# Attention with soft mixture of experts: a batch's turned logits and exponentials made around the first head's values

## The chip, the cores and the metric

One core of a Trainium2 chip runs the whole program. The metric is the device time of one launch in microseconds, the median of several runs; the profile is one execution of the same program, with the hardware profiler on. Five engines work side by side, each through its own queue in order: PE (matrix multiply), DVE (VectorE), ACT (ScalarE), POOL (GpSimd) and SP (which issues DMAs here). They wait for each other by semaphores.

## The reference, cut to what matters

Causal attention with a decay per position over 8 batches of 8 heads, 576 positions, 64 values a head; its output is the input of a soft mixture of 8 experts with 32 slots.

```python
# attention, for each batch and head
scores = q @ k.T / sqrt(D) + cum[:, None] - cum[None, :]      # cum = cumsum(log f)
attn = softmax(where(causal, -1e9, scores))
x = (attn @ v)            # -> (4608, 512): rows are tokens, columns head x value
# soft mixture of experts
logits = x @ phi                                              # 4608 x 32
d = exp(logits - logits.max(0)); d /= d.sum(0) + 1e-9          # over all tokens
slot_input = d.T @ x
slot_out = each expert's two layers on its 4 slots
c = exp(logits - logits.max(1)); c /= c.sum(1) + 1e-9          # over the slots
out = c @ slot_out
```

## The kernel before

The work is written out by hand: the order of the program's lines is the order of each engine's queue. The main loop runs over g, a pair of heads (32 pairs, 4 to a batch). I call one turn of it a slot. A slot holds, for pair g, the exact scores of both heads (`s2`, PE, into three PSUM banks `ring` in turn), their exponentials (`expo`, ACT, into `PTS`), the causal masks (`causal`, POOL), the values (`s3`, PE, 25 small matmuls a head, which the trace counts as 50, into the banks `pv`), and the normalization (`norm`, DVE). Between them stand a first pass of scores for heads further ahead (`s1`, PE, into PSUM tiles `s`) and their row maxima (`tops`, DVE), and the rounding of the keys and queries of pair g + 3 (`round_k`, `round_q`, ACT, from `RAW` into `WA` and `YA`). `load_qk(g + 3)` at the slot's start brings `RAW`; POOL makes the low parts (`low_k`, `low_q`).

The mixture's work for batch b is spread over the four slots after the batch's last pair; `b, w = divmod(g - 4, 4)`, so w counts them. In w = 0 `logits` makes the 32 logits of the batch's tokens, slots on partitions. In w = 1 `weigh` copies them to the tile `LG`, `mgroup` and `mtop` reduce them to a maximum per slot (`row`), `mcast` spreads it over the partitions (four small matmuls on PE into a bank of `ring`, then L405 and L407 on DVE), `weigh2` makes the exponentials `EX` (ACT), `total` adds up their sum, and `tokens` turns logits and exponentials so that tokens are on partitions: two transpositions of `LG` and two of `EX` on PE into the PSUM tile `tk`, and a copy of the turned exponentials to `LD` (ACT). L407 writes the negated maximum to column 192 of `LG`, which the second transposition of `LG` reads (columns 128 to 255). In w = 2 `combine(b, 0)` reduces and subtracts the row maximum of the turned logits (L475, L476, DVE, from `tk`), and `dispatch` multiplies the exponentials with x (PE). In w = 3 the other steps of `combine` follow.

`tk`, the tiles `s` and the logits take the three PSUM buffers of the pool `ps_s` in turn, in the order of the program. Three allocations after `tk` comes the tile of `s1(u0, 0)` of the next slot, so that matmul has to wait until everything that reads `tk` is done. All the dependencies are kept by the tile framework, for `tk` as one tile: a write to it waits for earlier reads of any part of it.

The end of a w = 1 slot, in order, before the change: the last `s1` and `s2`, `mcast`, `round_k`, `weigh2` and `total`, `round_q`, `s3` and `norm` of the first head, `s3` of the second head, `tokens`; the second head's `norm` comes in the next slot, and behind it `combine(b, 0)`.

Of the kernel before, what the change touches and what calls it, by code (L numbers as in the profile page):

```python
# [15 lines left out]
B, H, S, D = 8, 8, 576, 64  # L16
# [56 lines left out]
def attn_softmoe(ctx: ExitStack, tc: tile.TileContext, qk, v, f, phi, w1, w2, cst, out):  # L73
# [71 lines left out]
    st = {}  # L145
# [13 lines left out]
    def scratch(late, name):  # L159

        return turn() if late else ps_s.tile([P, 512], F32, name=name, tag="s")

    def turn():
        ring.append(ring.pop(0))
        return ring[-1]
# [10 lines left out]
    def round_k(g, *hs):  # L176
        if pair(g):
            for h in hs or range(2):
                nc.scalar.copy(WA[g % 3][0:64, S * h : S * h + S], RAW[g % 3][64:128, h])  # L179
# [35 lines left out]
    def s1(i, *which):  # L215

        if not head(i):
            return
        g, h = divmod(i, 2)
        ya, wa, m = YA[g % 3], WA[g % 3][:, S * h : S * h + S], TOP[g % 3]  # L220
        for n in which:
            bank, o, blk, j0, w = TOPS[n]
            if o == 0:
                st["top", i % 2, bank] = scratch(False, f"s{i}_{bank}")
            t = st["top", i % 2, bank]
            nc.tensor.matmul(  # L226
                t[:, o : o + w], ya[0:m, h, 128 * blk : 128 * blk + 128], wa[0:m, j0 : j0 + w], start=True, stop=True
            )
# [34 lines left out]
    def s2(i, *which):  # L263
        if not head(i):
            return
        g, h = divmod(i, 2)
        ya, wa, yb, wb, m = YA[g % 3], WA[g % 3], YB[g % 2], WB[g % 2], TOP[g % 3] + 1
        for n in which:
            bank, c, i0, w = SEGS[n]
            t, at = (turn(), 0) if n < 4 else st["bank"]  # L270

            n = 128 if c < 4 else 64
            o = t[0:n, at : at + w]
            at += w
            j0 = S * h + 128 * c
            nc.tensor.matmul(o, wa[0:m, j0 : j0 + n], ya[0:m, h, 64 + i0 : 64 + i0 + w], start=True, stop=False)  # L276
            nc.tensor.matmul(o, wb[:, j0 : j0 + n], yb[:, h, i0 : i0 + w], start=False, stop=True)  # L277
            st["bank"] = t, at
# [120 lines left out]
    def mcast(b):  # L399
        if not batch(b):  # L400
            return
        pm = turn()
        for j in range(4):
            nc.tensor.matmul(pm[32 * j : 32 * j + 32, 0:2], row, ones[0:1], start=True, stop=True)
        nc.vector.tensor_copy(st["mb", b][:, 1:2], pm[:, 0:1])  # L405
        if b < B - 1:
            nc.vector.tensor_scalar_mul(LG[:, 192:193], pm[:, 0:1], -1.0)  # L407
# [23 lines left out]
    def tokens(b, *ns):  # L431

        if not batch(b):
            return
        pm = turn() if b == B - 1 else scratch(False, f"tk{b}")
        for n in ns:
            src = (LG, EX)[n]
            nc.tensor.transpose(pm[:, 160 * n : 160 * n + 128], src[:, 0:128], ident)
            nc.tensor.transpose(pm[:, 160 * n + 128 : 160 * n + 256], src[:, 128:256], ident)
        if 0 in ns:  # L440
            st["tok", b] = pm
        if 1 in ns:
            copy = nc.scalar.copy if b < B - 1 else nc.vector.tensor_copy
            copy(LD, pm[:, 160:320].rearrange("p (t s) -> p t s", t=NBLK))
# [21 lines left out]
    def combine(b, step):  # L466

        if not batch(b):
            return
        ce = ctok[:, b]  # L470
        if step == 0:

            lt = st["tok", b][:, 0 : NBLK * NS].rearrange("p (t s) -> p t s", t=NBLK)
            sm = st["sm", b] = const.tile([P, 2, NBLK], F32, name=f"sm{b}", tag="sm", bufs=1)
            nc.vector.tensor_reduce(sm[:, 0], lt, axis=AX.X, op=ALU.max)  # L475
            nc.vector.tensor_tensor(ce, lt, wide(sm[:, 0]), op=ALU.subtract)  # L476
        elif step == 1:
            st["ce"] = turn()
            nc.scalar.activation(st["ce"][:, 0 : NBLK * NS].rearrange("p (t s) -> p t s", t=NBLK), ce, AF.Exp)
        else:  # L480
            sm, pm = st["sm", b], st["ce"]
            et, to = pm[:, 0 : NBLK * NS].rearrange("p (t s) -> p t s", t=NBLK), pm[:, NBLK * NS : NBLK * NS + NBLK]
            nc.vector.tensor_reduce(to, et, axis=AX.X, op=ALU.add)
            nc.vector.tensor_scalar_add(sm[:, 1], to, EPS)
            nc.vector.reciprocal(sm[:, 1], sm[:, 1])
            nc.vector.tensor_tensor(ce, et, wide(sm[:, 1]), op=ALU.mult)
# [208 lines left out]
    for g in range(1, NG):  # L695
        h0, h1 = 2 * g, 2 * g + 1
        u0, u1 = h0 + 3, h0 + 4
        b, w = divmod(g - 4, NPAIR)
        load_v(g + 1)
        if g > 0:  # L700
            load_qk(g + 3)
        if w == 1:
            weigh(b)
        low_q(h0 + 2)
        low_q(h1 + 2)
        s2(h0, 0)
        expo(h0, 0)
        norm(h0 - 1)
        if w == 1:
            mgroup(b)  # L710
        if w == 2:
            combine(b, 0)
        s1(u0, 2)
        tops(u0, 2)
        s2(h0, 1)
        expo(h0, 1)
        s1(u0, 3)
        tops(u0, 3)
        if g > 1:
            px(g - 1, 0)  # L720
        s2(h0, 2)
        expo(h0, 2)
        if g > 1:
            px(g - 1, 3)
        else:
            round_k(3, 0)
            round_q(3, 0)
        s1(u0, 0, 1)
        tops(u0, 0, 1)
        if g > 1:  # L730
            px(g - 1, 1)
        s2(h0, 3)
        if g > 1:
            xcopy(g - 1, (0,))
            xcopy(g - 1, (3,))
            px(g - 1, 2)
        s2(h0, 4)
        s1(u0, 4, 5)
        s2(h0, 5)
        expo(h0, 3)  # L740
        tops(u0, 4, 5)
        causal(h0)
        low_k(h0 + 2)
        if w == 1:
            mtop(b)
        s2(h1, 0)
        expo(h1, 0)
        if g == 1:
            for t in (0, 3, 1, 2):
                px(0, t)  # L750
            xcopy(0, (0,))
            xcopy(0, (3,))
        px(g - 1, 4)
        xcopy(g - 1, (1, 2))
        xcopy(g - 1, (4,))
        s1(u1, 2)
        tops(u1, 2)
        s2(h1, 1)
        expo(h1, 1)
        s1(u1, 3)  # L760
        tops(u1, 3)
        s2(h1, 2)
        expo(h1, 2)
        mturn(g + 1)
        mrows(g + 1)
        s1(u1, 0, 1)
        tops(u1, 0, 1)
        s2(h1, 3, 4)
        s1(u1, 4, 5)
        s2(h1, 5)  # L770
        expo(h1, 3)
        tops(u1, 4, 5)
        causal(h1)
        low_k(h1 + 2)
        if g == 1:
            round_k(3, 1)
            round_q(3, 1)
        load_cum(g + 3)
        dup_q(g + 2)
        dup_k(g + 2)  # L780
        if g == 29:
            sides[2].close()
            p2 = fresh(ctx, "p2", 2)
            wstream(RAW[30 % 3], *p2)
        if g == 30:
            sides[1].close()
            xp = ctx.enter_context(tc.tile_pool(name="xp", bufs=1))
            X.append(xp.tile([P, NBLK, 256], F32, name="X3"))
            p0 = fresh(ctx, "p0", 1)
            p1 = fresh(late, "p1", 3)  # L790
            wstream(RAW[31 % 3], *p0, *p1)
        if g == 31:
            sides[0].close()
            with tc.using_default_side("right"):
                tp = ctx.enter_context(tc.tile_pool(name="tp", bufs=1))
            cT = tp.tile([P, 26 * P], F32R, name="cT")
        if w == 1:
            mcast(b)
        if w == 3:
            combine(b, 1)  # L800
        if w == 2 and b < B - 2:
            dispatch(b, *range(NBLK))
        if g == NG - 1:
            st["lg", B - 1] = scratch(False, f"lg{B - 1}")
            nc.vector.memset(st["lg", B - 1][:, 128:192], -1.0e30)  # L805
        round_k(g + 3)
        if w == 1:
            weigh2(b)
            total(b)
        round_q(g + 3)  # L810
        if w == 3:
            combine(b, 2)
        s3(h0)
        norm(h0)
        if g == 31:
            wstream(PTS[:, 0:QW])
            split(0, 0)
            split(1, 0)
        s3(h1)
        if w == 0:  # L820
            logits(b, *range(NPAIR))
        if w == 1:
            tokens(b, 0, 1)
        if g >= 4 and g - 4 < NRES:
            wload(g - 4)
        if g == 28:
            wstream(RAW[29 % 3])
# [4 lines left out]
    b = B - 1  # L832
# [41 lines left out]
    pm = turn()  # L874
# [207 lines left out]
```

## Time and profile before

| | |
|---|---|
| median of 3 runs | 400.83 us (400.12 to 402.21) |
| the profiled execution | 401.76 us, of which the span of the engines' work is 400.1 us |
| main loop's length of a slot | 8.87 us (w = 3) to 11.12 us (w = 2 of batch 1) |
| busy PE, DVE, ACT, POOL | 380.7, 282.9, 262.5, 250.8 us |
| mean granted clock of PE | 0.983 |

In the prediction, a row of a timeline reads: start and length in us, engine, line of the kernel, operation, output<-inputs, shapes, count, and in brackets the engine's idle time before it with what ended it. PE is the matmul itself, PEld the load of its stationary operand, which overlaps other matmuls; rows that follow each other without a gap may overlap, as the engines are pipelined. A row of a table by windows reads: the stretch and its length, the engine's busy time in it and its instructions, the clock, the busy share of the DMA engines, GB/s.

### The profile page before, as it was taken

The page shows a single profiled execution, that of the slowest core. Times are in us where ns is not written, and L with a number is a line of the kernel's source. Part 1 is how long each engine was busy: PE and PEld are TensorE (multiplying, and loading weights), DVE is VectorE, ACT ScalarE, POOL GpSimd, SP SyncE. Part 2 cuts the span into 40 slices and gives each one's busy share as a digit, 9 for nine tenths or more (in the row PEclk, how much of TensorE's full clock was granted, in tenths as well). Part 3 has the DMA queues.
Part 4 walks back from the last instruction along what each step waited for, and adds up shares of the span by engine and source line. Part 5 has one row for each costly group of instructions (what it writes and reads, how often), then busy time and mean ns, then how long its engine had stood idle before and what let it go on. Part 6 is the DMA issues. An engine that isn't in the chain of part 4 may idle for free.

```text
span 400.1 us, 15146 instructions
## 1 busy us (share of the span) xinstructions
PE 380.7 (95%) x5843; PEld 333.1 (83%) x5843; DVE 282.9 (71%) x1130; ACT 262.5 (66%) x675; POOL 250.8 (63%) x341
## 2 busy tenths in 40 slices
PE   8999999999999999999999999999999998999880
PEld 7889999999989999999999989999999885444540
DVE  7878887879767978787888778877878444312571
ACT  8859777767776777668777786777776542240450
POOL 4697887878767877787878777877787520000000
PEclk9999999999999999999999999999999999999985
DMA  6866767777777777777777677877675699999798
GB/s 206 209 159 161 231 169 207 205 210 209 206 208 207 209 207 208 210 208 207 209 208 225 201 209 204 225 209 214 199 185 151 240 343 350 409 407 387 247 378 333
DMA packets 34744, 93.72 MB, mean 234 GB/s; under 512 B 4282, under 2 KB 9072, under 8 KB 34672
## 3 DMA queue, kind: packets, MB, share of 16 engines
q1 hardware_dynamic: 34672, 92.75, 75.1%
q8 instruction: 46, 0.75, 0.8%
q14 instruction: 26, 0.21, 0.2%
HBM read 63.93 MB, written 9.73 MB: 184 GB/s over the span
## 4 chain that ended last, share of the span: by engine, by line
PE 90%; DMA 3%; ACT 2%; DVE 1%; issue 1%; SPq 0%; DVEq 0%; ACTq 0%
PE pv L311 25%; PE ring L276 13%; PE s L226 12%; PE ring L277 12%; PE pv L338 4%; PE pv L936 4%; PE more L899 4%; PE lg L374 3%; PE ring L491 3%; PE ring L1016 2%; PE ds L455 2%; DMA RAW<-in_qk 2%; DMA out<-RAW 1%; PE ring L684 1%; PE pv L249 1%; ACT PTS L283 1%
## 5 line engine op out<-in xcount | busy, mean ns | idle before, releaser
L283 ACT ACTIVATE PTS<-ring 128x320 f32<-128x320 f32 (+2 forms) x256 | 119.5, 513 | 61.3 <-PE ring L277 33.8
L239 DVE CUSTOM_DVE_ANT_0 s<-s,mask 128x320 f32<-128x320 f32 (+4 forms) x320 | 137.4, 449 | 5.3 <-PE s L226 0.8
L276 PE MATMUL ring<-YA,WA 67*128 67x320 f32 (+9 forms) x384 | 121.8, 330 | 0.0
L277 PE MATMUL ring<-YB,WB 128*128 128x320 f32 (+4 forms) x384 | 110.7, 296 | 0.0
L311 PE MATMUL pv<-V,PTS 128*64 128x65 f32 x3200 | 104.3, 223 | 0.7 <-ACT mr L258 0.7
L311 PEld LDWEIGHTS pv<-V,PTS 128*64 128x64 f32 x3200 | 99.6, 137 | 3.4 <-ACT mr L258 1.2
L226 PE MATMUL s<-WA,YA 66*128 66x288 f32 (+9 forms) x384 | 98.6, 312 | 1.7 <-ACT PTS L283 1.3
L205 POOL TENSOR_TENSOR WB<-RAW,WB 64x576 fp32r<-64x576 f32 x64 | 90.3, 1410 | 11.0 <-DMA WB<-WA 5.0
L210 POOL TENSOR_TENSOR YB<-RAW,YA 64x576 fp32r<-64x576 f32 x64 | 89.3, 1414 | 2.5
L276 PEld LDWEIGHTS ring<-YA,WA 67*128 67x128 f32 (+3 forms) x384 | 69.7, 183 | 5.4 <-issue 2.1
L277 PEld LDWEIGHTS ring<-YB,WB 128*128 128x128 f32 (+1 forms) x384 | 69.9, 182 | 0.0
L226 PEld LDWEIGHTS s<-WA,YA 66*128 66x128 f32 (+1 forms) x384 | 63.0, 190 | 7.8 <-ACT PTS L283 2.4
L294 POOL TENSOR_SCALAR_AFFINE_SELECT PTS<-PTS 128x128 f32<-128x128 f32 (+1 forms) x128 | 31.3, 265 | 35.2 <-ACT PTS L283 32.3
L239 DVE DVE_READ_ACCUMULATOR2_ANT MT<- 128x1 f32 x372 | 52.5, 141 | 0.0
L291 POOL TENSOR_SCALAR_AFFINE_SELECT PTS<-PTS 128x384 f32<-128x384 f32 x64 | 33.3, 520 | 25.8 <-ACT PTS L283 22.8
L179 ACT CAST WA<-RAW 64x576 fp32r<-64x576 f32 x64 | 40.1, 669 | 12.8 <-DMA RAW<-in_qk 12.3
L338 PE MATMUL pv<-cs,X 128*128 128x128 f32 x155 | 42.1, 277 | 0.2 <-DVE lg L805 0.2
L239 DVE CUSTOM_DVE_ANT_0 s<-s,mask,MT 128x288 f32<-128x288 f32 x62 | 32.6, 526 | 11.2 <-PE s L226 2.2
L184 ACT CAST YA<-RAW 64x576 fp32r<-64x576 f32 x63 | 39.4, 669 | 0.4
L326 DVE TENSOR_SCALAR rl<-pv 128x5 f32<-128x5 f32 x64 | 10.5, 164 | 33.2 <-PE pv L311 32.7
L331 DVE TENSOR_TENSOR X<-pv,rl 128x320 f32<-128x320 f32 (+1 forms) x65 | 31.5, 486 | 2.4 <-DMA YA<-mr 0.3
L362 ACT COPY XT<-pv 128x128 f32<-128x128 f32 (+1 forms) x124 | 28.6, 292 | 0.0
(184 smaller groups left out, 353.5 us busy)
## 6 DMA issues: line engine op xcount, KB each, us to landing
w<-in_w SPq DMA_DIRECT2D x46, 512.0 KB
RAW<-in_qk SPq DMA_DIRECT2D x31, 576.0 KB
V<-in_v SPq DMA_DIRECT2D x32, 325.0 KB
YB<-YA SPq DMA_DIRECT2D x30, 288.0 KB
WB<-WA SPq DMA_DIRECT2D x30, 288.0 KB
p<-in_w SPq DMA_DIRECT2D x7, 512.0 KB
out<-p SPq DMA_DIRECT2D x6, 512.0 KB
out<-RAW SPq DMA_DIRECT2D x9, 256.0 KB
```

The source lines that it names most:

```text
L179: nc.scalar.copy(WA[g % 3][0:64, S * h : S * h + S], RAW[g % 3][64:128, h])
L184: nc.scalar.copy(YA[g % 3][0:64, h, 64:640], RAW[g % 3][0:64, h])
L205: nc.gpsimd.tensor_tensor(t[0:64], RAW[g % 3][64:128, h], t[64:128].bitcast(F32), op=ALU.subtract)
L210: nc.gpsimd.tensor_tensor(YB[g % 2][64:128, h], RAW[g % 3][0:64, h], YA[g % 3][0:64, h, 64:640].bitcast(F32), op=ALU.subtract)
L226: nc.tensor.matmul(t[:, o : o + w], ya[0:m, h, 128 * blk : 128 * blk + 128], wa[0:m, j0 : j0 + w], start=True, stop=True)
L239: nc.vector.tensor_tensor_reduce(out=t[:, o : o + w], in0=t[:, o : o + w], in1=mask[:, m0 : m0 + w], scale=1.0, scalar=top if n == 3 else ...
L276: nc.tensor.matmul(o, wa[0:m, j0 : j0 + n], ya[0:m, h, 64 + i0 : 64 + i0 + w], start=True, stop=False)
L277: nc.tensor.matmul(o, wb[:, j0 : j0 + n], yb[:, h, i0 : i0 + w], start=False, stop=True)
L283: nc.scalar.activation(PT[i % 2][:, SEG_O[bank] : SEG_O[bank] + at], t[:, 0:at], AF.Exp, scale=0.125)
L291: nc.gpsimd.affine_select(d3, d3, pattern=[[0, 3], [1, 128]], compare_op=ALU.is_ge, fill=0.0, base=0, channel_multiplier=-1)
L311: nc.tensor.matmul(o[64 * u : 64 * u + 64, t, :], PT[i % 2][:, at : at + 64], V[:, g % 2, c, 65 * h : 65 * h + 65], start=(c == 0), stop=( ...
L338: nc.tensor.transpose(pm[:, 0:128], x[:, t, 128 * (p % 2) : 128 * (p % 2) + 128], ident)
```

## The change

In the slots with w = 1, all batches but the last: `mcast` moves up, in front of the last `s1` and the end of `s2`; `weigh2` and `total` move in front of `round_k`; the logits' two transpositions (`tokens(b, 0)`) and `combine(b, 0)`, which was in the next slot, come in front of `round_k` and of the first head's values; the exponentials' transpositions and their copy to `LD` (`tokens(b, 1)`) come between the two heads' values, in front of `round_q`. `tokens` takes the PSUM tile in its first call and uses it again in the second. The last batch, which is done behind the loop, is as before. From `tokens` on, line numbers after the change are 5 higher.

```diff
-        pm = turn() if b == B - 1 else scratch(False, f"tk{b}")
+        if b == B - 1:
+            pm = turn()
+        elif 0 in ns:
+            pm = scratch(False, f"tk{b}")
+        else:
+            pm = st["tok", b]
...
         if w == 1:
             mgroup(b)
-        if w == 2:
-            combine(b, 0)
...
         s2(h1, 3, 4)
+        if w == 1:
+            mcast(b)
         s1(u1, 4, 5)
         s2(h1, 5)
...
-        if w == 1:
-            mcast(b)
...
-        round_k(g + 3)
         if w == 1:
             weigh2(b)
             total(b)
-        round_q(g + 3)
+            tokens(b, 0)
+            combine(b, 0)
+        round_k(g + 3)
         if w == 3:
             combine(b, 2)
         s3(h0)
         norm(h0)
+        if w == 1:
+            tokens(b, 1)
+        round_q(g + 3)
...
         if w == 0:
             logits(b, *range(NPAIR))
-        if w == 1:
-            tokens(b, 0, 1)
```

On PE, the end of batch 1's w = 1 slot before the change (`s` the first pass of scores, `ring` the exact ones and the cast maximum, `pv` the values, `tk` the turned tile; the shape is the output's):

```order
L226 MATMUL s_3_1870<-WA_94,YA_93 128x448
L226 MATMUL s_3_1870<-WA_94,YA_93 128x64
L276 MATMUL ring_151<-YA_89,WA_90 64x64
L277 MATMUL ring_151<-YB_87,WB_88 64x64
L404 MATMUL ring_152<-cs,row 32x2 x4
L311 MATMUL pv_148<-V,PTS 64x65 x25
L311 MATMUL pv_149<-V,PTS 64x65 x25
L438 MATMUL tk_1952<-cs,LG 128x128
L439 MATMUL tk_1952<-cs,LG 128x128
L438 MATMUL tk_1952<-cs,EX 128x128
L439 MATMUL tk_1952<-cs,EX 128x128
```

The same place after it:

```order
L404 MATMUL ring_152<-cs,row 32x2 x4
L226 MATMUL s_3_1876<-WA_94,YA_93 128x448
L226 MATMUL s_3_1876<-WA_94,YA_93 128x64
L276 MATMUL ring_151<-YA_89,WA_90 64x64
L277 MATMUL ring_151<-YB_87,WB_88 64x64
L443 MATMUL tk_1894<-cs,LG 128x128
L444 MATMUL tk_1894<-cs,LG 128x128
L311 MATMUL pv_148<-V,PTS 64x65 x25
L443 MATMUL tk_1894<-cs,EX 128x128
L444 MATMUL tk_1894<-cs,EX 128x128
L311 MATMUL pv_149<-V,PTS 64x65 x25
```

The cast moved up by four matmuls, the logits' transpositions to right behind the last scores, the exponentials' between the heads' values.

On DVE, the same slot before, from the last maximum of the first pass to the first normalization (`MT` the maxima, `mb` and `LG` the cast maximum):

```order
L239 ISA s_3_1870,MT_115<-s_3_1870,mask 128x448
L239 ISA MT_115 128x1
L239 ISA s_3_1870,MT_115<-s_3_1870,mask 128x64
L405 COPY mb_1796<-ring_152 128x1
L407 TENSOR_SCALAR LG<-ring_152 128x1
L326 TENSOR_SCALAR rl_1923<-pv_148 128x5
```

And after:

```order
L405 COPY mb_1796<-ring_152 128x1
L407 TENSOR_SCALAR LG<-ring_152 128x1
L239 ISA s_3_1876,MT_115<-s_3_1876,mask 128x448
L239 ISA MT_115 128x1
L239 ISA s_3_1876,MT_115<-s_3_1876,mask 128x64
L480 TENSOR_REDUCE sm_1897<-tk_1894 128x5
L481 TENSOR_TENSOR ctok<-tk_1894,sm_1897 128x160
L326 TENSOR_SCALAR rl_1927<-pv_148 128x5
```

The two small operations behind the cast come before the last maximum, and the combine (L475, L476 before) between that and the first normalization.

On ACT, one piece of the difference at the end of the same slot (WA is written by `round_k`, YA by `round_q`):

```order
-L179 CAST WA_90<-RAW_95 64x576 x2
 L414 ACTIVATE EX,mb_1796<-LG,mb_1796 128x192
 L418 ACTIVATE mb_1796<-mb_1109,mb_1796 128x1
 L427 ACTIVATE lrun<-lrun,mb_1796 128x1
-L184 CAST YA_89<-RAW_95 64x576 x2
-L444 COPY LD<-tk_1952 128x160
+L179 CAST WA_90<-RAW_95 64x576 x2
+L449 COPY LD<-tk_1894 128x160
+L184 CAST YA_89<-RAW_95 64x576 x2
```

The exponential passed the first rounding, and the copy to `LD` the second one.

## The prediction

> **What bounds the kernel now.** I read the page first, its first and its fourth part: busy time by engine, and the chain that ended last.
>
> ```profile
> span 400.1 us, 15146 instructions
> PE 380.7 (95%) x5843; PEld 333.1 (83%) x5843; DVE 282.9 (71%) x1130; ACT 262.5 (66%) x675; POOL 250.8 (63%) x341
> PE 90%; DMA 3%; ACT 2%; DVE 1%; issue 1%; SPq 0%; DVEq 0%; ACTq 0%
> ```
>
> PE is busy for 95% of the span and is 90% of the chain. The change gives PE the same matmuls in another order, so it can win only what PE loses to waits in the slots that it touches, and can lose only by new waits there. Next I cut the loop into slots, from the first score matmul of one pair to that of the next, and asked for PE's busy time in each: rows 1 and 2 are value slots (w = 1) of batches 0 and 1, rows 3 to 8 the slots after them (w = 2) of batches 0 to 5, the last one w = 3.
>
> ```profile
> core 0: us, PE busy (x), PEclk, DMA share, GB/s
> 64.70:74.13 9.43, 9.43 (x156) 1.00 0.68 203
> 103.37:113.16 9.79, 9.65 (x156) 1.00 0.67 197
> 74.13:84.19 10.06, 10.06 (x186) 1.00 0.76 214
> 113.16:124.28 11.12, 10.32 (x185) 1.00 0.71 198
> 152.90:163.28 10.38, 10.31 (x185) 1.00 0.75 211
> 191.91:202.16 10.25, 10.25 (x186) 1.00 0.77 214
> 230.76:241.58 10.82, 10.32 (x186) 1.00 0.74 210
> 270.19:280.58 10.39, 10.35 (x185) 1.00 0.77 215
> 84.19:93.06 8.87, 8.87 (x144) 1.00 0.71 213
> ```
>
> The six w = 2 slots hold the same work, yet take 10.06 to 11.12 us. Above 10.06 stand 1.06, 0.32, 0.19, 0.76 and 0.33, together 2.66 us. The w = 1 slot of batch 1 is 0.36 longer than batch 0's. So 3.02 us is all that can be won, 0.75% of the time. What the lost time waits for is seen around 113 us, in timelines of ScalarE, VectorE and PE (batch 1):
>
> ```profile
> 111.10 1.24 ACT L179 CAST WA<-RAW 64x576 fp32r<-64x576 f32 x2 [1.26 <-DMA RAW<-in_qk]
> 112.37 0.46 ACT L414 ACTIVATE EX<-LG,mb 128x192 f32<-128x192 f32 x1
> 113.43 1.23 ACT L184 CAST YA<-RAW 64x576 fp32r<-64x576 f32 x2
> 114.56 0.28 ACT L444 COPY LD<-tk 128x160 f32<-128x160 f32 x1
> 114.88 0.33 DVE L475 TENSOR_REDUCE sm<-tk 128x5 f32<-128x160 f32 x1 [1.46 <-ACT LD L444]
> 115.23 0.33 DVE L476 TENSOR_TENSOR ctok<-tk,sm 128x160 f32<-128x160 f32 x1
> 115.71 0.47 PE L226 MATMUL s<-WA,YA 66*128 66x320 f32 x2 [0.80 <-ACT PTS L283]
> ```
>
> The load of the pair three ahead (RAW) landed late, so ScalarE began its rounding 1.26 us late; the exponential, the second rounding and the copy to LD followed. VectorE's combine stood behind that copy, and PE's top-score matmul, which takes over the PSUM buffer of tk (three buffers in turn), stood behind the combine. The profile puts PE's 0.80 us on ScalarE; the buffer rotation and the times (L476 ends at 115.56, PE starts 0.15 later) say that it was L476. This is a delay even where the load is on time:
>
> ```profile
> 188.96 1.24 ACT L179 CAST WA<-RAW 64x576 fp32r<-64x576 f32 x2
> 192.43 0.28 ACT L444 COPY LD<-tk 128x160 f32<-128x160 f32 x1
> 193.10 0.33 DVE L476 TENSOR_TENSOR ctok<-tk,sm 128x160 f32<-128x160 f32 x1
> 193.54 0.30 PEld L226 LDWEIGHTS s<-WA,YA 66*128 66x128 f32 x2
> ```
>
> No wait stands before that rounding (batch 3), the copy to LD still comes late, and PE's load follows L476's end (193.43) by 0.11: this is the slot with 0.19 lost.
>
> **The change, part by part.** *The exponential ahead of the first rounding, the combine ahead of the first normalization: the gain.* After the change L476's work ends in the value slot, and tk's last reader is the copy to LD. With batch 3's times ScalarE is free at 188.96, runs the exponential and its three small followers (1.06, from 112.37 to 113.43 in batch 1) and the rounding (1.24): about 191.26, then the copy, 191.55. PE wants the buffer in the next slot, some 2 us later (it took it at 193.54 with 0.19 of delay). So 2.66 us go, and batch 1's 0.36 too, since its exponential no longer stands behind the late load. The combine's 0.66 us moves into idle time of VectorE, which sits 0.52 us before each normalization:
>
> ```profile
> 111.05 0.17 DVE L326 TENSOR_SCALAR rl<-pv 128x5 f32<-128x5 f32 x1 [0.52 <-PE pv L311]
> ```
>
> *The logits' transpositions ahead of the first values: the price.* The second of them reads columns 128 to 255 of LG, so also column 192, which L407 writes from the cast maximum. Before, 3 us of value matmuls lay between L407 and that transposition. Now only PE's cast (moved up), two top-score matmuls and the last scores do, and VectorE is behind PE there:
>
> ```profile
> 109.05 0.24 PE L404 MATMUL ring<-cs,row 1*32 1x2 f32 x8
> 109.22 3.25 PE L311 MATMUL pv<-V,PTS 128*64 128x65 f32 x100
> 109.41 0.67 DVE L239 CUSTOM_DVE_ANT_0 s<-s,mask 128x448 f32<-128x448 f32 x1
> 110.32 0.15 DVE L405 COPY mb<-ring 128x1 f32<-128x1 f32 x1
> 110.39 0.15 DVE L407 TENSOR_SCALAR LG<-ring 128x1 f32<-128x1 f32 x1
> 112.39 0.33 PE L438 MATMUL tk<-cs,LG 128*128 128x128 f32 x1
> 112.56 0.27 PE L439 MATMUL tk<-cs,LG 128*128 128x128 f32 x1
> ```
>
> VectorE begins the 448-wide top at 109.41. L405 now takes that place, and L407 ends 0.22 later (110.32 to 110.54 in the rows): 109.63. PE can have it 0.15 after that, as after L476: 109.78. PE would come to the second transposition where the values began, 109.22, plus the 0.17 between the two transpositions: 109.39. It waits 0.39 us, which is the gap between the value matmuls' start and the 448-wide top's start (0.19) plus 0.20. The first, the latest and the last of the other batches:
>
> ```profile
> 70.54 3.25 PE L311 MATMUL pv<-V,PTS 128*64 128x65 f32 x100
> 70.74 0.67 DVE L239 CUSTOM_DVE_ANT_0 s<-s,mask 128x448 f32<-128x448 f32 x1
> 188.31 3.25 PE L311 MATMUL pv<-V,PTS 128*64 128x65 f32 x100
> 188.68 0.67 DVE L239 CUSTOM_DVE_ANT_0 s<-s,mask 128x448 f32<-128x448 f32 x1
> 305.62 3.25 PE L311 MATMUL pv<-V,PTS 128*64 128x65 f32 x100
> 305.81 0.67 DVE L239 CUSTOM_DVE_ANT_0 s<-s,mask 128x448 f32<-128x448 f32 x1
> ```
>
> The gaps are 0.20, 0.37 and 0.19; six of the seven lie between 0.19 and 0.22, so the wait is 6 x 0.40 + 0.57 = 2.97 us. Its low end is a release that costs nothing: 7 x 0.15 less, 1.9; its high end adds a whole weight load, 0.14 a batch, if nothing hides it any more, 3.95:
>
> ```profile
> 112.45 0.14 PEld L439 LDWEIGHTS tk<-cs,LG 128*128 128x128 f32 x1
> ```
>
> I take 2.97, since both L476's releases show 0.11 to 0.15. All of PE's queue stands behind it, the values first.
>
> *The exponentials' transpositions between the two heads' values.* The program makes them wait for the exponential and for the combine's last read of tk. Counted from the 448-wide top's old start: L405 and L407 0.15, the two tops 0.91 (109.41 to 110.32), reduce and subtract 0.68 (114.88 to 115.56), release 0.15: 1.89. PE: second transposition at 0.37, 0.11 for itself, half of the 3.17 between the values' start and the transposition: 2.07. It is ready 0.18 us before it is needed, in every batch, as both sums start from the same event. Cost nothing; without this cover 0.1 to 0.2 a batch.
>
> *The roundings, the copy to LD.* The first rounding starts 1.06 later where the load is on time. Its readers, the copies to the second tile and the top scores of that pair, come in the next slot. The copy to LD now waits on PE with the second rounding and the next slot's exponential queued behind it: in batch 3 the transpositions would stand at 188.68 + 2.07 = 190.75, LD would be copied from about 191.26 to 191.55 and the rounding done by 192.8, while the next slot's first scores begin only after the second head's values, at 190.75 + 0.22 + 1.59 = 192.56. No DMA is issued at another place, SP's and POOL's queues keep their order, and the cast and the four transpositions cost PE the same 0.56 (9.43 less the 8.87 of w = 3) wherever they stand.
>
> *Sum.* Profiled execution 401.76, 1.66 of it around the span: 401.76 - 3.02 + 2.97 = 401.71. The median of the runs is 400.83, 0.93 below. If the median run has just fewer of the late landings, it has little left to win and the changed kernel stands at 401.7; if its 0.93 lies elsewhere, at 400.8. I take 401.2 between them: no change that can be measured (0.5%, 2.0 us, is about what a measurement of this kernel can tell).
>
> **A rule beside the rows.** In the rows the combine began 0.04 us after the copy to LD ended (114.84 to 114.88), though it reads other columns of tk. The Trainium skill, "PSUM — Partial Sum Buffer", section "PSUM bank collisions raise a hardware error", says that accesses of two engines to one bank and quadrant must be kept apart by semaphores, two reads included, whatever the columns. The trace agrees, by that 0.04. By that rule sharing tk speaks against this change: exponentials can't be written beside logits that are being read, which is the 1.89 against 2.07 above; the sum would stay as it is while the first is smaller, and past that point rival (1) would hold.
>
> **The rivals.** (1) *Second wait.* The combine ends after the first head's values, so PE waits a second time for tk. For it: the margin is only 0.18 us and built from five durations; against it: all were measured on this engine in this order. If the combine came 0.3 us later, 7 x 0.12 = 0.8 more: 402.0. (2) *No price.* VectorE reaches L405 in time, or the wait on L407 falls into time that PE loses anyway: 401.2 - 2.97 = 398.2. Against it: in all seven batches the 448-wide top starts 0.19 to 0.37 after the values. (3) *Price without gain, the slower side.* In a usual run the loads land on time and each w = 2 slot loses only batch 3's 0.19, so 5 x 0.19 = 0.95 is won and 2.97 paid: 400.83 + 2.0 = 402.9. It decides where the stalls of the w = 2 slots sum to under 1 us; for it speaks that the profiled execution is 0.93 above the median, against it that one in three runs (402.21) was longer still. (4) *It does not do what it says*: the copy to LD, now behind a late rounding, holds tk as the combine did. Batch 1: landing 111.10 + 1.24 + 0.28 = 112.62, wanted at 115.71 - 0.80 = 114.91; the load would have to come 2 us later still. Time: 401.2 + 2.7 = 403.9.
>
> **How the numbers follow.** Forecast 0.72; (1) 0.11; (2) 0.06; (3) 0.09; (4) 0.02. Slower by over 0.5% are half of (3), (4), and a little of (1): 0.08. Faster is (2), 0.06. The rest, 0.86, is within 0.5%. The range reaches from 399.4, the low price of 1.9 with the whole gain against the median (400.83 - 3.02 + 1.9 = 399.7) and a little below, to 402.8, just short of (3).
>
> **What would show it.** In the changed profile: the w = 2 slots all at 10.0 to 10.1 and the copy to LD before the second rounding (gain right); PE's weight load of the second logits transposition 0.4 us after the first one, ended by VectorE's L407, seven times (price right); no wait at the exponentials' transposition (margin right). I am wrong if that wait is under 0.2 us or if w = 2 slots still differ by more than 0.2.

## The result, and the profile after

The changed kernel takes 404.94 us (404.68 to 405.22, 6 runs), the one before 400.88 (400.12 to 402.21, 6 runs): ratio 1.0095, 95% interval 1.008 to 1.011. It is slower by 4 us (1%), outside my range; I had forecast no change that can be measured. The profiled execution took 405.22, its span is 403.5 against 400.1. One of the four executions of a later run, `no_wait`, took 465.71 us at a granted clock of 0.749 and is left out of that run's figures.

The page, parts 1 and 4: PE has 3.9 us more of busy time with the same 5843 instructions.

```profile
span 403.5 us, 15153 instructions
PE 384.6 (95%) x5843; PEld 333.6 (83%) x5843; DVE 283.5 (70%) x1130; ACT 263.2 (65%) x675; POOL 250.8 (62%) x341
PE 87%; DMA 5%; DVE 2%; ACT 2%; POOL 2%; issue 1%; SPq 0%; DVEq 0%; ACTq 0%; POOLq 0%
```

The same cut by slots as in the prediction, PE alone: two w = 1 slots, six w = 2 slots, one w = 3.

```profile
64.99:75.24 10.25, 10.19 (x156) 1.00 0.70 202
104.52:114.79 10.27, 10.18 (x156) 1.00 0.69 199
75.24:85.34 10.10, 10.10 (x185) 1.00 0.69 199
114.79:124.89 10.10, 10.10 (x185) 1.00 0.73 205
154.44:164.54 10.10, 10.10 (x185) 1.00 0.67 199
194.03:204.11 10.08, 10.08 (x184) 1.00 0.68 197
233.55:243.63 10.08, 10.08 (x184) 1.00 0.73 205
273.10:283.18 10.08, 10.08 (x185) 1.00 0.69 202
85.34:94.22 8.88, 8.88 (x145) 1.00 0.70 210
```

The gain came: all w = 2 slots are level, 60.54 us in sum against 63.02, and batch 1's w = 1 slot (10.27) is no longer longer than the others by 0.36. The price is twice what I had set: the seven w = 1 slots went from 66.36 to 71.87. With 0.43 in the other slots and before the loop this makes the 3.46 us between the two spans. The end of batch 1's w = 1 slot, PE's weight loads:

```profile
109.81 0.15 PEld L404 LDWEIGHTS ring<-cs,row 1*32 1x32 f32 x8
109.98 0.30 PEld L226 LDWEIGHTS s<-WA,YA 66*128 66x128 f32 x2
110.43 0.14 PEld L443 LDWEIGHTS tk<-cs,LG 128*128 128x128 f32 x1
110.84 0.14 PEld L444 LDWEIGHTS tk<-cs,LG 128*128 128x128 f32 x1 [0.28 <-DVE LG L407]
111.10 1.59 PEld L311 LDWEIGHTS pv<-V,PTS 128*64 128x64 f32 x50
112.76 0.14 PEld L443 LDWEIGHTS tk<-cs,EX 128*128 128x128 f32 x1
112.82 0.14 PEld L444 LDWEIGHTS tk<-cs,EX 128*128 128x128 f32 x1
113.13 1.59 PEld L311 LDWEIGHTS pv<-V,PTS 128*64 128x64 f32 x50 [0.17 <-issue]
114.79 0.19 PEld L276 LDWEIGHTS ring<-YA,WA 67*128 67x128 f32 x1
```

The wait for L407 is there (0.28). But the values, which ran through in 3.17 before, now take 111.10 to 112.76 and 113.13 to 114.79, 1.66 a head, and 0.31 pass from the last transposition's load to the values' return, where the next slot's scores followed 0.11 behind it before. None of that is a wait for another engine. The profile shows a part, the 0.17 in the last bracket, as "issue" before the weight load, a time in which the engine waited for nothing that the profile shows; the rest looks like busy PE (10.19 of the 10.25 us of the first row above).

### The profile page after: what moved, and what is told of

It is laid out like the page before. It is cut to its first block, busy times and chain, and to the rows that moved or that the text cites. A ratio compares the mean times of both kernels' runs of the same rounds, so it can differ in the third digit from the quotient of the medians.

```text
span 403.5 us, 15153 instructions
## 1 busy us (share of the span) xinstructions
PE 384.6 (95%) x5843; PEld 333.6 (83%) x5843; DVE 283.5 (70%) x1130; ACT 263.2 (65%) x675; POOL 250.8 (62%) x341
## 4 chain that ended last, share of the span: by engine, by line
PE 87%; DMA 5%; DVE 2%; ACT 2%; POOL 2%; issue 1%; SPq 0%; DVEq 0%; ACTq 0%; POOLq 0%
PE pv L311 24%; PE ring L276 13%; PE s L226 11%; PE ring L277 11%; PE pv L338 4%; PE pv L941 4%; PE more L904 4%; PE ring L496 3%; DMA RAW<-in_qk 3%; PE lg L374 3%; PE ds L460 2%; PE ring L1021 2%; DMA out<-RAW 1%; ACT PTS L283 1%; PE ring L689 1%; DMA YA<-mr 1%
## 5 line engine op out<-in xcount | busy, mean ns | idle before, releaser
L311 PE MATMUL pv<-V,PTS 128*64 128x65 f32 x3200 | 105.8, 223 | 0.8 <-ACT mr L258 0.8
```

The lines of the kernel that those rows point to most:

```text
L311: nc.tensor.matmul(o[64 * u : 64 * u + 64, t, :], PT[i % 2][:, at : at + 64], V[:, g % 2, c, 65 * h : 65 * h + 65], start=(c == 0), stop=( ...
```

## The experiments

Each ratio below is to the kernel before, run on the same chip; the lengths of slots come from one profile a run.

Theory "switch": PE loses time whenever it changes between the values (64 columns stationary) and other work, so the cast in a new place and the stop between the heads cost by themselves. Rival "wait": the transpositions cost the same anywhere, and the excess comes from the wait for VectorE and what follows it.

**The stop measured by itself.** `dummies` is the kernel before with

```diff
+def dummy(n, cols):
+    for _ in range(n):
+        nc.tensor.transpose(pv[1][0:cols, 384:512], ident[:, 0:cols], ident)
```

called at different places of the w = 3 slots.

> The kernel before, with extra transpositions of the identity, read by nobody, in the w = 3 slots alone (8.88 us each without them): batch 0 one with 128 columns between the two heads' values, batch 1 one with 128 columns behind the second head's values, batch 2 one with 64 columns between the heads, batch 3 one with 32 columns between the heads, batch 4 two with 128 columns between the heads, batch 5 one with 128 columns in front of the first head's values. Theory 'switch' (PE loses time at each change between the 64-column values and 128-column work): batch 0 +0.45, batch 1 +0.15, batch 2 +0.11 or less, batch 3 +0.35, batch 4 +0.56, batch 5 +0.25. Rival 'wait' (a transposition costs its 0.11 wherever it stands, and the changed kernel lost only by waiting): +0.11 in all, +0.22 in batch 4.

The w = 3 slots of batches 0 to 5 (the second row is batch 1's, the third the slot behind it, into which that transposition's cost runs):

```profile
84.28:93.55 9.27, 9.27 (x146) 1.00 0.69 212
124.22:133.18 8.96, 8.96 (x145) 1.00 0.67 205
133.18:143.66 10.48, 10.48 (x176) 1.00 0.78 221
163.85:173.09 9.24, 9.24 (x145) 1.00 0.67 205
203.06:212.30 9.24, 9.24 (x146) 1.00 0.70 207
242.28:251.66 9.38, 9.38 (x146) 1.00 0.68 203
281.76:290.79 9.03, 9.03 (x146) 1.00 0.65 199
```

Between the heads one transposition costs 0.39, and one of 64 or of 32 columns 0.36, two 0.50; in front of the values 0.15 (batch 5). Batch 1's transposition, behind the second head, costs 0.08 in its slot and some 0.17 in the next, whose neighbours are 10.31, so 0.25 in all. "Wait", with 0.11 in every place, does not hold. "Switch" does in the main: but it had 0.25 in front of the values and 0.15 behind them, the other way round, and had not foreseen that 64 columns cost as much as 128. So `dummies2` put other forms there:

> The kernel before with an extra PE instruction, read by nobody, between the two heads' values of the w = 3 slots (8.88 us without): batch 0 a matrix product of the values' own form (64 columns stationary, 65 moving), batch 1 a product of 32 columns stationary and 2 moving, batch 2 a product of 128 columns stationary and 65 moving, batch 3 two products of the values' form on both halves, batch 4 a transposition of 128 by 128, batch 5 a transposition of 64 by 64. 'The tile size makes the stop': batch 0 and 3 under +0.08, batch 1 +0.3, batch 2 +0.35, batch 4 +0.37, batch 5 small. 'The transposition makes it': batches 0 to 3 under +0.1, batches 4 and 5 +0.37. 'Any stop of the row of values does': all +0.3 or more.

The w = 3 slots of batches 0 to 5:

```profile
84.25:93.23 8.98, 8.98 (x147) 1.00 0.72 212
123.64:132.81 9.17, 9.17 (x147) 1.00 0.75 206
163.05:172.43 9.38, 9.38 (x146) 1.00 0.69 206
202.43:211.43 9.00, 9.00 (x149) 1.00 0.69 208
241.43:250.70 9.27, 9.27 (x146) 1.00 0.69 205
280.69:289.88 9.19, 9.19 (x145) 1.00 0.63 199
```

Products of the values' own form cost 0.10 (one) and 0.12 (two); the tiny product of 32 columns 0.29, one of 128 columns 0.50 (the trace counts it as two matmuls, and two transpositions cost 0.50 as well), the transpositions 0.39 and 0.31. None of the three theories holds whole. A product stops the row of values when its width differs from theirs; a transposition does so even with 64 columns. That any interruption would do it is refuted by the 0.10.

**The parts of the change.** `cast_alone`: the kernel before with only

```diff
         s2(h1, 3, 4)
+        if w == 1:
+            mcast(b)
...
-        if w == 1:
-            mcast(b)
```

> The kernel before with the cast of the maximum alone moved up, in front of the last first-pass scores, as in the changed kernel; nothing else moves. 'Switch': the 32-column products now stand between two pieces of full-width work, and the values lose the short way from the cast to them: w = 1 slots at 9.43 + 0.17 = 9.60, the w = 2 slots as before, 1.2 us more, 402.1. 'Wait': a product costs the same wherever it stands, 9.43, 400.9.

It took 402.13 us (ratio 1.0032, 1.0021 to 1.0044). The w = 1 slots have 9.59 to 9.60, as "switch" said; the first of them:

```profile
64.61:74.20 9.59, 9.59 (x156) 1.00 0.69 202
```

`ex_late` is the changed kernel with

```diff
-        if w == 1:
-            tokens(b, 1)
         round_q(g + 3)
...
         if w == 0:
             logits(b, *range(NPAIR))
+        if w == 1:
+            tokens(b, 1)
```

> The changed kernel with the exponentials' two transpositions and their copy behind the second head's values again; the logits' transpositions and the combine stay early. 'Switch': the w = 1 slots go from 10.25 to about 9.95 (the values of both heads run through, 3.18 instead of 2 x 1.66, and one return to the values goes), 7 x 0.3 = 2.1 us less, 402.8. 'Wait': nothing changes, 404.9, as the wait for the cast maximum stays.

It took 402.22 us (1.0033, 1.0020 to 1.0046). The first two w = 1 slots:

```profile
64.52:74.47 9.95, 9.87 (x156) 1.00 0.68 202
103.69:113.63 9.94, 9.87 (x157) 1.00 0.68 197
```

The w = 2 slots behind them became shorter too, 10.03 where the changed kernel has 10.08 to 10.10, which "switch" had not said.

`no_wait`: the changed kernel with the running maximum in a column that is not turned.

```diff
-    LG = const.tile([P, 256], F32, name="LG")
+    LG = const.tile([P, 257], F32, name="LG")
...
-LG[:, 0:193] if b < B - 1
+LG[:, 0:257] if b < B - 1
...
-nc.vector.tensor_scalar_mul(LG[:, 192:193], pm[:, 0:1], -1.0)
+nc.vector.tensor_scalar_mul(LG[:, 256:257], pm[:, 0:1], -1.0)
```

> The changed kernel with the running maximum in a column of its own (256) that no transposition reads, so that the second transposition of the logits does not wait for VectorE's write; the batch's maximum then reads 257 columns instead of 193. 'Switch': only the wait of 0.34 goes, the w = 1 slots go from 10.25 to 9.9, 402.6. 'Wait': the whole excess of 0.82 goes, 9.43, 399.2.

Two of its w = 1 slots and what lies from the loop's last slot (pair 31) on, which I call behind the loop; the last row is the kernel before's:

```profile
64.67:74.64 9.97, 9.97 (x156) 1.00 0.71 202
103.87:113.84 9.97, 9.97 (x156) 1.00 0.68 198
318.73:402.02 83.29, 66.94 (x818) 0.94 0.94 348
317.73:400.05 82.32, 67.41 (x818) 0.92 0.94 352
```

The slots do what "switch" says (9.97; 9.9 was said, as I had put the wait at 0.34), yet the time is 403.73, not 402.6 (1.0076, 1.0058 to 1.0094): behind the loop it takes 83.29 where the kernel before and the changed one take 82.32. `no_wait_ex_late` has both edits (LG 264 columns wide):

> The changed kernel without the wait for the cast maximum (running maximum in a column of its own, the tile 264 columns wide) and with the exponentials' transpositions behind the second head's values. 'Switch': w = 1 slots at 9.95 - 0.30 = 9.65, still 0.22 above 9.43 for the cast among full-width work and the return from the logits' transpositions to the values; 7 x 0.30 less than the 402.22 of the kernel with the wait, 400.1. 'Wait': 9.43, 398.5.

```profile
64.69:74.34 9.65, 9.65 (x156) 1.00 0.69 202
103.51:113.16 9.65, 9.65 (x156) 1.00 0.66 197
```

The slots are at 9.65 as expected. The time is 400.88, that of the kernel before (400.95; 0.9998, 0.9986 to 1.0010) and not 400.1, as the part behind the loop took 83.75. So each batch's 0.82 (10.25 - 9.43) is made of 0.17 for the cast, 0.28 for the wait (10.25 - 9.97), 0.30 for the exponentials between the heads (10.25 - 9.95) and 0.05 for the logits' turn in front of the values (9.65 - 9.60): 0.80 of it. "Wait" alone, which asked for 9.43 without the wait, is refuted.

`all_between` is the changed kernel with the cast back in its old place (the edit of `cast_alone` undone) and all four transpositions and the combine behind `norm(h0)`:

```diff
             total(b)
-            tokens(b, 0)
-            combine(b, 0)
...
         norm(h0)
         if w == 1:
-            tokens(b, 1)
+            tokens(b, 0, 1)
+            combine(b, 0)
```

> The changed kernel with the cast maximum at its old place and all four transpositions and the combine between the two heads' values. The wait is gone and one stop between the heads is left. 'Switch': w = 1 slots at 9.75 (values 1.66, four transpositions 0.28, return 0.31, values 1.66), 7 x 0.5 less, 401.4. 'Wait': 9.43, 399.2.

The w = 1 slots came out right (9.78), the time did not: 404.29 (1.0089, 1.0073 to 1.0106). In the slot behind, batch 1:

```profile
113.31 0.28 ACT L449 COPY LD<-tk 128x160 f32<-128x160 f32 x1
113.62 0.33 DVE L480 TENSOR_REDUCE sm<-tk 128x5 f32<-128x160 f32 x1 [1.19 <-ACT LD L449]
114.64 0.49 DVE L331 TENSOR_TENSOR X<-pv,rl 128x320 f32<-128x320 f32 x1
115.19 0.33 PE L338 MATMUL pv<-cs,X 128*128 128x128 f32 x1 [0.31 <-DVE X L331]
```

The combine, now behind the copy to LD again, stood ahead of the second head's normalization, and PE waited 0.31 for the normalized values: the w = 2 slots of batches 1 to 5 have 10.58. That comes from where this kernel puts the combine; neither theory had it.

**Is there a version that keeps the gain?** `exp_early` is the kernel before with only the exponential moved.

```diff
-        round_k(g + 3)
         if w == 1:
             weigh2(b)
             total(b)
+        round_k(g + 3)
```

> The kernel before with one part of the change alone: the exponential and the sum in front of the first rounding; the cast, the transpositions and the combine stay. Theory (the w = 2 slots lose time because the combine stands behind the copy to LD, and that behind both roundings): only the share of late landings goes, w = 2 slots at 10.05 to 10.3, 0.5 to 2 us less than before, 399.5 to 400.4. Rival (the late exponential was the cause of the w = 2 stalls): all of them at 10.05, 398.7.

It took 404.26 us (1.0081, 1.0061 to 1.0101), worse than theory and rival had it. Around batch 1's w = 2 slot:

```profile
111.01 0.46 ACT L414 ACTIVATE EX<-LG,mb 128x192 f32<-128x192 f32 x1 [0.70 <-DVE mb L405]
112.17 1.25 ACT L179 CAST WA<-RAW 64x576 fp32r<-64x576 f32 x2
114.59 0.28 ACT L444 COPY LD<-tk 128x160 f32<-128x160 f32 x1
114.90 0.33 DVE L475 TENSOR_REDUCE sm<-tk 128x5 f32<-128x160 f32 x1 [1.01 <-ACT LD L444]
115.73 0.47 PE L226 MATMUL s<-WA,YA 66*128 66x320 f32 x2 [0.70 <-ACT PTS L283]
```

With the cast at its old place the exponential waits 0.70 for VectorE's L405, both roundings behind it, and every w = 2 slot becomes 10.6 to 11.0, in batches where nothing had been late too. It shows the chain from the other side: what comes late on ScalarE reaches PE through LD, the combine and tk. `copy_all` adds to `exp_early` one copy of logits and exponentials together (only the line that matters is shown):

```diff
-    copy(LD, pm[:, 160:320]...)
+    nc.scalar.copy(LDW, pm[:, 0:320]...)      # LD = LDW[:, 1]; combine reads LDW[:, 0]
```

> The kernel before with the early exponential, and with logits and exponentials both copied from tk by one ScalarE copy (320 columns), from which the combine reads later; no transposition and no cast moves. Theory (what is to be won is the release of tk, and the changed kernel lost it by moving PE's work): w = 1 slots at 9.43, w = 2 slots at 10.05, 2 us less than the kernel before, 398.7. Rival (the early place of the transpositions is needed to release tk in time): w = 2 slots as before, 10.05 to 11.1, 400.5.

It took 407.19 us (1.0150, 1.0129 to 1.0171), worse than both theories. It has `exp_early`'s delay, and the combine, which waits for the copy at the head of VectorE's queue, now delays the top scores' maxima (w = 2 slots of 10.88 in batch 0 and 11.12 to 11.33 in batches 1 to 5). `copy_late` has `copy_all`'s copy, the exponential at its old place and the combine where VectorE idles:

```diff
-        if w == 2:
-            combine(b, 0)
         s1(u0, 2)
...
         s3(h0)
+        if w == 2:
+            combine(b, 0)
         norm(h0)
```

> The kernel before with every instruction of PE and both roundings and the exponential at their old places: ScalarE's one copy to LD takes the turned logits too (320 columns instead of 160, 0.41 us instead of 0.28), and the combine reads that copy at the end of the w = 2 slot, in front of the first head's normalization, instead of tk at its start. Theory (tk was held too long by a combine that stood behind the copy, and the gain does not need PE's work to move): w = 1 slots at 9.43, w = 2 slots at 10.05 or within 0.2 of it where the load lands late, 398.8. Rival (the copy itself, late behind both roundings, holds tk as long): w = 2 slots as before, 400.9.

Three of the rows, the w = 1 slot of batch 0, the w = 2 slot of batch 1, and behind the loop:

```profile
64.60:74.05 9.45, 9.45 (x157) 1.00 0.67 202
112.69:122.72 10.03, 10.03 (x186) 1.00 0.81 226
314.89:399.30 84.41, 68.28 (x818) 0.91 0.92 343
```

The loop ends 2.8 us earlier than in the kernel before (314.89 against 317.73) with no PE work moved: the release of `tk` can be had without the price. But 400.78 is no gain (0.9994, 0.9982 to 1.0006): the part behind the loop, 84.41 instead of 82.32, took most of it back in the profile. Two runs asked why. `wide_alone` changes no instruction:

```diff
-    LG = const.tile([P, 256], F32, name="LG")
+    LG = const.tile([P, 416], F32, name="LG")
```

> The kernel before with the tile LG 160 columns wider (640 bytes a partition) and not an instruction changed: every tile that is allocated behind it lies elsewhere in SBUF, as in the kernel with the wide copy. Theory (the part behind the loop loses about 1 us by where its tiles lie): behind the loop 83.3 instead of 82.3, 401.7. Rival (it lost because the loop ended earlier and the output transfers were the bound): 82.3, 400.8.

It took 401.77 us (1.0020, 1.0007 to 1.0033). Behind the loop (the second row is `copy_all`'s, which has another tile wider by as much):

```profile
316.93:400.34 83.41, 66.96 (x818) 0.94 0.94 347
322.37:405.64 83.27, 67.69 (x818) 0.91 0.93 348
```

The place of the tiles is worth about 1 us. `copy_in_place` needs no space, since the turned logits go straight to the combine's own tile:

```diff
 copy(LD, pm[:, 160:320]...)
+if b < B - 1:
+    nc.scalar.copy(ctok[:, b], pm[:, 0:160]...)   # combine reads ctok[:, b], late as above
```

> As the wide copy with the late combine, but with no new space: a second ScalarE copy takes the turned logits straight to the place in ctok where the combine works on them; all tiles lie as before. w = 1 slots at 9.43, w = 2 slots at 10.05 to 10.2. Theory (place of the tiles): 82.3 behind the loop, 398.9. Rival (output transfers are the bound once the loop ends earlier): 83 to 84 behind the loop, 400.3.

It took 399.31 us (398.87 to 401.16, 11 runs), ratio 0.9961, 0.9948 to 0.9975: 0.4% less than the kernel before, where the changed kernel takes 0.95% more. Its profiled execution is its slowest run, with two w = 2 slots delayed (the second row is one of them):

```profile
112.82:122.87 10.05, 10.05 (x186) 1.00 0.82 224
151.62:162.19 10.57, 10.40 (x185) 1.00 0.72 203
316.20:399.45 83.25, 68.01 (x818) 0.93 0.93 348
```

In both the first rounding had waited 1.0 us and more for its load, and PE's top scores waited 0.4 us and more for the second copy, which stands behind the two roundings: a late load still reaches PE here.

83.25 behind the loop with all tiles in their old place says that the end of the loop matters too, at least in that run. The profiles side by side part the two causes further. Before, after, `cast_alone`, `ex_late`, `all_between` and `exp_early` have their tiles in the old place and end the loop between 317.73 and 321.19; all six take 82.30 to 82.33 behind it. `no_wait` and `copy_all`, with a wider tile, end it at 318.73 and 322.37 and take 83.29 and 83.27: here the place alone makes the 1.0. `copy_in_place`, tiles in place, ends it at 316.20 and takes 0.9 more. `no_wait_ex_late` and `copy_late` have a wider tile and an early end (315.85 and 314.89), with 1.4 and 2.1 more. `wide_alone`'s loop ended at 316.93, so its 83.41 may hold some of both. These are single profiles, and what about the place it is, and why an early end of the loop is lost, stays open.

## Why the prediction was wrong

- *The gain*: right. All w = 2 slots stand at 10.08 to 10.10 (said: 10.0 to 10.1), 2.5 us less.
- *The wait for L407*: right in kind, and it was too large: seven waits of 0.26 to 0.31 before that weight load, 1.9 us in sum against 2.97, the low end of what I had given. The second load stands 0.39 to 0.45 behind the first, as said. What was too large is, first, the release: I had set 0.15 from L476, and the load follows L407's end by 0.05 in all seven batches, 0.7 us in sum. Second, L407 ended 0.17 to 0.23 behind PE's arrival at the second transposition (0.17 behind the first), where I had 0.24 to 0.42, taken from the old order. That the moved cast, which makes PE later by 0.17 in `cast_alone`, did this fits, but no run shows it by itself.
- *The second wait for tk*: right that it does not come; the exponentials' transpositions follow the first head's values without a wait in all seven batches. In batch 1 the combine ended at 112.26, 0.5 us before their load at 112.76.
- *"The cast and the four transpositions cost PE the same 0.56 wherever they stand"*: this is the step that failed, and with it the opening sentence that the change "can lose only by new waits". They cost 0.52 a batch more (0.17 the cast, 0.30 the stop between the heads, 0.05 the logits), 3.6 us in seven batches. I had read 0.56 from one order and taken it for a property of the instructions. A hint stood in the profile of before: the first of the four transpositions, behind the values, takes 0.17 to the second (112.39, 112.56), where the later ones take 0.11 (191.66, 191.77, 191.88 in batch 3).
- *The sum*: for the profiled execution I had 401.71, and it took 405.22, 3.5 more. The stop's 3.6 and 0.2 of gain that did not come, less the 1.1 by which the wait was too large, give 2.7. The other 0.8, of which 0.43 lies outside the w = 1 and w = 2 slots, has no cause to its name.
- The rivals missed it too. Slower was forecast as price without gain; gain and price were both there, and the price had a second half. Rivals (3) and (4), with 402.9 and 403.9, came nearer by the number alone: the gain that they denied was there.

The Trainium skill, "TensorEngine Tiling (Array Packing)", section "Key Properties", states that changing the tiling mode drains TensorE. The runs agree: 0.10 for a product in the values' own form, 0.29 for a much smaller one of another width. The Trainium skill, "TensorEngine Tiling (Array Packing)", section "Restrictions", states that column tiling disables the transpose mode for FP32 input. That a transposition with the values' own 128 rows and 64 columns costs 0.36 fits this, though no run shows in which mode it ran.

## What to carry to other kernels

An instruction's price on PE depends on its neighbours: before you move small matmuls or transpositions into a row of products of another tile width, price the change of width on either side, not the instruction. Most of it appears as busy time and none as a wait for another engine, so measure it with a dummy in a slot where nothing else happens. And when a buffer is held too long, first look for a reader to move: one more copy by an engine that has time, and the reader moved behind it, gained 1.5 us here, where reordering PE's queue lost 4.

## What the runs showed that was not expected

- A transposition of 128, 64 or 32 columns between the two heads' values costs the same 0.36 to 0.39 us; a second one behind it adds 0.11.
- A tile 640 bytes a partition wider, with no instruction changed, costs 1.0 us (0.2%). Behind the loop, where the output is written, its profile takes 83.4 instead of 82.3.
- A loop that ends 2.8 us earlier was worth nothing in `copy_late`: the last part then took 84.4, 1.0 of it probably for the place of its wider tile, the rest open.
